# Moving the Wq and Wk loads to another queue, and four small reorderings ahead of them, in a kernel that sums a memory attention and an MLP

## The chip, the cores and the metric

The kernel runs on one core of one Trainium2 chip. The metric is the device time of one execution in microseconds (us). A core has TensorE (PE in the profile, with PEld for its weight loads), VectorE (DVE), ScalarE (ACT), GpSimd (POOL) and SyncE (SP). A DMA is started by an instruction in the queue of one of these engines, here SP or POOL, and every queue is worked off in order: an instruction that waits holds up all that stand behind it. The profile shows SP's own instructions as "SPq".

## The reference

Input x is 2048 rows of 1024 in bfloat16. Two branches work on its layer norm and are added to it.

```python
xn = _layernorm(x)
out = x + A(xn, mem0, Wq, Wk, Wv, Wo) + B(xn, w1, w2, w3, w4)

# A: 64 segments of 32 tokens, one after the other; 8 memory rows are carried along
for s in range(64):
    h = concat([mem, xn[32*s : 32*s+32]])             # 40 rows
    q, k, v = h @ Wq, h @ Wk, h @ Wv                  # 32 heads of 128
    p = softmax(where(mask, q @ k.T * 128**-0.5, -1e9))
    o = (p @ v) @ Wo
    mem, out_s = o[:8], o[8:]

# B
h  = gelu(layernorm(xn) @ w1)                         # 1024 -> 1024
hs = shift_tokens(h) @ w2                             # four column groups, shifted by +1, -1, +2, -2 rows
x1 = xn + hs
B  = x1 + gelu(layernorm(x1) @ w3) @ w4               # 1024 -> 3584 -> 1024
```

## The kernel before

The kernel doesn't carry the memory from segment to segment. It estimates the memory rows of all segments at once from sums over the segments, uses them for one parallel pass over all 2048 tokens, checks at the end that the rows which the pass gave agree with the estimate, and only if they don't runs a serial version (the branch behind line 868, not taken here). TensorE, SP and POOL work in the order in which the program is written; in the first two stages DVE and ACT do too.

1. **First MLP matmul (lines 222 to 363).** `load_x` (L233) and the quarters of w1 (L237) are queued on SP. For each of 16 tiles of 128 rows, `norm_stats` computes mean and variance on DVE (L256 for the left half, L259 for the right, L260, L261) and the inverse roots on POOL (L262). `norm2` makes the twice normed tile xn2 (L271 on DVE for tiles 0 to 7, L273 on ACT from tile 8). `transposes` turns tiles 0 to 7 on TensorE (L290) and copies them out (L294 on ACT, L292 on DVE for the second half of tile 0); later tiles are turned by a DMA (L274). `stage1` multiplies with w1 (L301), eight column blocks `co` of eight matmuls each, and runs gelu on ACT (L303). The dictionary `between` says after which `co` other work is put: `prep(n)` is norm2 of tile n, the statistics of n + 1 and the once normed tile n - 2 (L280, stored by L281). Tiles 0 to 3 go one at a time, then two at a time.
2. **Second MLP matmul (lines 365 to 391).** w2, layer norm of x1, transposed by DMA (L388).
3. **w3 and w4 (lines 393 to 556).** Four rounds `tb` over 512 rows each: 28 groups of eight matmuls with w3 (L522), then four row tiles of 56 matmuls with w4 (L545). At the start SP loads w4 in seven chunks (L418) between DMA transposes of xn (L409, `seg_sums`) whose sums over segments go into `xb` (L412). `mem_start` (L423 to L428) turns the 8 memory rows with eight small matmuls (L426), writes them into `MZ` (L427) and adds their sum to the first column of `xb` (L428). "Speculative" units (`spec_step`) are put between the big matmuls: `unit_vb` multiplies `xb` with Wv (L438) and is the first reader of `xb`. DVE adds each w4 product to `R1` (L546), which SP loads (L513) and POOL adds to x (L541).
4. **Values (lines 565 to 608).** All tokens times Wv (L577), written to memory (L584). At its end SP loads the weights of the first pass (L600) and Wq of the second (L603).
5. **Attention (lines 611 to 809).** Five blocks of 12 to 16 segments (4 tiles each, 5 in blocks 3 and 4), each with eight passes `hg` over four heads. A pass has eight projections, four with Wq and four with Wk (`proj`, L650, 64 matmuls together), and for every tile an "S" item and an "O" item. S (`scores`): four matmuls (L665), mask (L667), exp (L669), sums (L671), reciprocal (L673), product Pn (L677), and a DMA transpose PT<-Pn issued by SP (L680). O (`outputs`): four matmuls with the values V (L689), copied out by ACT (L690, L692). `tick` advances an estimated clock after each projection, starts S items when due and O items 10 us (`LAT`) after their S.
   The loads for a pass are made by `stage_loads` one pass ahead: two tiles `wt` from a pool of four (tag "w"), so that a load waits until TensorE has used the tile of two passes before; 512 KB halves (L737), then V (`load_values`, L635 to L643). They are put in a list `loads`, of which each `tick` issues one. After six of the eight projections of pass 1 of a block come the output projections of the block before (`Out.piece`, L708): for each of them POOL loads `Rt` (L706) and stores the result (L715), which waits for DVE (L714). At the start of pass 2, `block_setup` loads the next block's tokens `hTb` (L623) on POOL.

Of the kernel before, what the change touches and what calls it, by code (L numbers as in the profile page):

```python
# [77 lines left out]
def kernel(  # L78
# [16 lines left out]
    nc = tc.nc  # L95
# [6 lines left out]
    w1_v = B_w1.rearrange("(k p) n -> p k n", p=P)  # L102
# [90 lines left out]
    with tc.manual_schedule(engines={mybir.EngineType.PE, mybir.EngineType.SP, mybir.EngineType.Pool}), ExitStack() as actx:  # L193
# [6 lines left out]
        with ExitStack() as bctx:  # L200
# [13 lines left out]
            with ExitStack() as hctx:  # L214
# [7 lines left out]
                with ExitStack() as p0:  # L222
                    big = p0.enter_context(tc.tile_pool(name="p0big", bufs=1))
                    ring = p0.enter_context(tc.tile_pool(name="p0ring", bufs=3))
                    w1_sb = big.tile([P, KT, D], BF16)
# [4 lines left out]
                    def load_x(n):  # L230
                        if n < NT:
                            xts[n] = ring.tile([P, D], BF16, tag="xt", bufs=7, name=f"xt{n}")
                            nc.sync.dma_start(xts[n][:], x_v[:, n, :])  # L233

                    load_x(0)
                    for c0, c1 in ((0, 256), (256, 512), (512, 1024)):
                        nc.sync.dma_start(w1_sb[:, :, c0:c1], w1_v[:, :, c0:c1])  # L237
                        if c0 == 0:
                            load_x(1)
                    for n in range(2, 7):  # L240
                        load_x(n)
# [5 lines left out]
                    def norm_stats(n, part=None):  # L247

                        if n >= NT:
                            return  # L250
                        xt = xts[n]
                        if n not in stats:
                            stats[n] = [ring.tile(shape, F32, tag=tag, bufs=6, name=f"{tag}{n}") for tag, shape in (("st", [P, 2, 6]), ("mv", [P, 2]), ("ab", [P, 2]), ("rr", [P, 2]), ("nm2", [P, 1]))]
                        st, mv, ab, rr, nm2 = stats[n]
                        if part in (None, 0):
                            nc.vector.bn_stats(st[:, 0, :], xt[:, 0:512])  # L256
                        if part == 0:
                            return
                        nc.vector.bn_stats(st[:, 1, :], xt[:, 512:1024])  # L259
                        nc.vector.bn_aggr(mv[:], st[:])  # L260
                        nc.vector.scalar_tensor_tensor(ab[:], epsm[:], mv[:, 1:2], epsa[:], op0=ALU.mult, op1=ALU.add)  # L261
                        nc.gpsimd.tensor_tensor(rr[:], ab[:], neghalf[:], op=ALU.pow)  # L262
                        if n >= NPE:
                            nc.gpsimd.tensor_scalar(nm2[:], mv[:, 0:1], rr[:, 1:2], -1.0, op0=ALU.mult, op1=ALU.mult)
# [61 lines left out]
                    def tr(n, half, on_dve=False):  # L326
                        transposes(xn2s[n], tiles2[n - n % 2], n % 2, half, on_dve)
# [8 lines left out]
                    nc.gpsimd.memset(hTB[:, :, S + 2:S + 4], 0.0)  # L336
                    load_consts(4)
                    for n in range(1, NPE):
                        norm_stats(n + 1, 0)
                        norm2_of(n)  # L340
                        norm_stats(n + 1, 1)
                        if n > 1:
                            norm1(n - 2)
                        if n < 4:
                            stage1(n - 1, 1, tiles2[(n - 1) // 2 * 2], {5: [lambda n=n: tr(n, 0)], 6: [lambda n=n: tr(n, 1)]}, (n - 1) % 2)
                    stage1(3, 1, tiles2[2], {4: [lambda: tr(4, 0)], 5: [lambda: tr(4, 1)], 6: [lambda: tr(5, 0)], 7: [lambda: tr(5, 1)]}, 1)

                    def prep(n):
                        norm2_of(n)
                        norm_stats(n + 1)  # L350
                        norm1(n - 2)

                    for n0 in range(4, NT, 2):
                        between = {c: [] for c in range(KT)}
                        if n0 + 4 < NT:
                            between[2] += [lambda n0=n0: prep(n0 + 4)]
                            between[5] += [lambda n0=n0: prep(n0 + 5)]
                        if n0 == 4:
                            for c in range(4):
                                between[1 + 2 * c // 2 + (c > 1)] += [lambda c=c: tr(6 + c // 2, c % 2)]  # L360
                        stage1(n0, 2, tiles2[n0], between)
# [31 lines left out]
            with ExitStack() as p3:  # L393
# [29 lines left out]
                def mem_start():  # L423
                    ps9 = psum3.tile([P, KT, M + 1], F32, tag="vr")
                    for k in range(KT):
                        nc.tensor.matmul(ps9[:, k, :], m0[:, k * P:(k + 1) * P], eye9[:], start=True, stop=True)  # L426
                    nc.vector.tensor_copy(MZ[:, :, 0:M], ps9[:, :, 0:M])  # L427
                    nc.vector.tensor_tensor(xb[:, :, 0:1], ps9[:, :, M:M + 1], xb[:, :, 0:1], op=ALU.add)  # L428
# [59 lines left out]
                def spec_load(depth=1):  # L488
                    while units and len(pending) < depth:
                        u, i = units.pop(0)  # L490
                        pending.append(u(i))
                        if u is unit_g and i == 7:
                            pending.append(unit_thr)
# [23 lines left out]
                for tb in range(4):  # L517
                    depth = 1 if tb < 2 else 2
                    for f in range(FT):
                        ps = psum.tile([P, 512], F32, tag="mm", bufs=4)  # L520
                        for k in range(KT):
                            nc.tensor.matmul(ps[:].rearrange("p (n t) -> p n t", t=P), w3_sb[:, k, f * P:(f + 1) * P], xn3T[tb][:, :, k, :], start=(k == 0), stop=(k == KT - 1))  # L522
                        nc.scalar.activation(h3T[:, f, :], ps[:], ACTF.Gelu_apprx_tanh)  # L523
                        if tb > 0 and f % 7 == 6:
                            spec_step(depth)
                    if tb == 0:
                        spec_load()
                    if tb == 3:
                        w3ctx.close()
                        early = actx.enter_context(tc.tile_pool(name="aearly", bufs=2, side="right"))  # L530
                        vctx = ExitStack()
                        vph = vctx.enter_context(tc.tile_pool(name="vph", bufs=1, side="right"))
                        xT = vph.tile([P, NT, KT, P], BF16)
                    for j in range(4):
                        n = tb * 4 + j
                        R1, xt = r1s.pop(n)
                        load_r1(n + 1)
                        if tb == 3:
                            for m in range(4 * j, 4 * j + 4):
                                nc.sync.dma_start_transpose(xT[:, m], xn_v[:, m, :])  # L540
                        nc.gpsimd.tensor_tensor(R1[:], R1[:], xt[:], op=ALU.add)  # L541
                        for ch in range(2):
                            ps = psum.tile([P, 512], F32, tag="mm", bufs=4)
                            for f in range(FT):
                                nc.tensor.matmul(ps[:], h3T[:, f, j * P:(j + 1) * P], w4_sb[:, f, ch * 512:(ch + 1) * 512], start=(f == 0), stop=(f == FT - 1))  # L545
                            nc.vector.tensor_tensor(R1[:, ch * 512:(ch + 1) * 512], ps[:], R1[:, ch * 512:(ch + 1) * 512], op=ALU.add)  # L546
                        if n == NT - 1:
                            while pending or units:
                                spec_step(depth)
                        elif n > 0:  # L550
                            spec_step(depth)
                        else:
                            mem_start()
                        if n == NT - 2:
                            load_wv()
                        nc.gpsimd.dma_start(R_v[:, n, :], R1[:])
# [8 lines left out]
            for hg in range(8):  # L565
                cs_ = slice(hg * 512, (hg + 1) * 512)
# [155 lines left out]
        loads = []  # L722
# [5 lines left out]
        def stage_loads(Bs, hg, ready=()):  # L728

            cs_ = slice(hg * 512, (hg + 1) * 512)  # L730
            ws = [(w, None) for w in ready]
            ws += [(wtile(), src) for src in (Wq_v, Wk_v)[len(ready):]]
            (wq, _), (wk, _) = ws
            Vs = [qkv.tile([P, len(B["tiles"]), 512], BF16, tag="V", bufs=3, name=f"V{B['b']}") for B in Bs]
            for w, src in ws[len(ready):]:
                for k0 in (0, 4):
                    loads.append(lambda w=w, src=src, k0=k0: nc.sync.dma_start(w[:, k0:k0 + 4, :], src[:, k0:k0 + 4, cs_]))  # L737
            for B, V in zip(Bs, Vs):
                loads.append(lambda B=B, V=V: load_values(B, V, hg))
            return wq, wk, Vs  # L740
# [21 lines left out]
        for gi_, group in enumerate(groups):  # L762
# [3 lines left out]
            for hg in range(8):  # L766
                cs_ = slice(hg * 512, (hg + 1) * 512)
# [100 lines left out]
    with tc.If(cond > 0):  # L868
        with ExitStack() as fctx:
# [18 lines left out]
            with tc.For_i(0, NSEG, 1) as i:  # L888
# [6 lines left out]
                for hg in range(8):  # L895
                    cs_ = slice(hg * 512, (hg + 1) * 512)
# [100 lines left out]
```

## Time and profile before

| | |
|---|---|
| median of 7 runs | 1527.56 us (1526.19 to 1532.76) |
| the profiled execution's own time | 1526.44 us |
| its span, first to last instruction | 1524.5 us |
| TensorE busy | 1513.4 us of the span; granted clock 0.999 |
| DVE, ACT, POOL busy | 545.9, 506.3, 178.9 us |
| matmuls of the attention: L650, L708 | 509.5, 225.2 us busy |
| matmuls of the values: L577 | 221.2 us busy |
| matmuls of the MLP: L522, L545 | 195.5, 196.0 us busy |
| DMA | 274.20 MB, mean 180 GB/s |

The span is what the trace covers; 1.9 us of the profiled execution's time lie outside it. Times inside the trace are counted from the start of the span. "Idle before" an instruction is the time for which its engine had nothing in work, and the name behind the arrow is what ended it. A matmul's end is modelled and about 0.17 us later than the point at which the next matmul can start, so that the time lost in a gap of TensorE is better taken from start to start, less the regular step between two matmuls of the same shape (0.216 us for 512 columns, by the 1024 of L577 in 221.2 us, and about 0.055 us for 128 columns).

### The profile page before, as it was taken

Reading aid. Unit: us, or ns where it says so; the run is one execution under the profiler, and the core shown is the slowest. Engines: PE = TensorE matmul, PEld = TensorE weight load, DVE = VectorE, ACT = ScalarE, POOL = GpSimd, SP = SyncE. Lnnn points to the kernel's source line nnn. Section 1 sums busy time; section 2 is a strip of 40 time slices with the busy share of each in tenths; the row PEclk is TensorE's granted clock in tenths of the full one; section 3 lists DMA queues with packets and bytes.
Section 4 is the critical chain, followed back from the end, with each engine's and each line's share of the span. In section 5 each row is a group of like instructions: output and inputs, shape, how many; then the busy total and the mean of one; then the engine's idle time right before and its main releaser. Section 6 shows DMA issues by size and latency. Waiting matters only on the chain.

```text
span 1524.5 us, 24352 instructions
## 1 busy us (share of the span) xinstructions
PE 1513.4 (99%) x9853; PEld 809.0 (53%) x9853; DVE 545.9 (36%) x1137; ACT 506.3 (33%) x1147; POOL 178.9 (12%) x248
## 2 busy tenths in 40 slices
PE   9999999999999999999999999999999999999998
PEld 7844444444444444444465645664665555445555
DVE  7383320000200122211145624650664266416542
ACT  5533203103012011111256614650663266326630
POOL 5232030221211231100000010001000100010001
PEclk9999999999999999999999999999999999999999
DMA  8799963452452977532499956992997389828611
GB/s 267 172 251 298 246 213 118 146 187 83 145 156 75 235 259 256 204 123 79 131 245 236 242 129 177 241 236 78 242 234 196 110 223 215 193 72 212 174 44 55
DMA packets 305435, 274.20 MB, mean 180 GB/s; under 512 B 153787, under 2 KB 273104, under 8 KB 305064
## 3 DMA queue, kind: packets, MB, share of 16 engines
q1 hardware_dynamic: 283144, 189.92, 49.8%
q0 software_dynamic: 22032, 82.63, 15.5%
q8 instruction: 79, 1.29, 0.4%
q14 instruction: 36, 0.29, 0.1%
q10 hardware_dynamic: 144, 0.07, 0.0%
HBM read 190.98 MB, written 46.19 MB: 156 GB/s over the span
## 4 chain that ended last, share of the span: by engine, by line
PE 93%; SPq 3%; DMA 3%; DVE 0%; ACT 0%; issue 0%; POOL 0%; POOLq 0%; DVEq 0%
PE ps L650 30%; PE pso L708 15%; PE ps L577 14%; PE ps L545 11%; PE ps L522 10%; PE ps L375 4%; PE ps L301 3%; SPq L409 2%; PE psS L665 2%; PE psO L689 2%; DMA PT<-Pn 1%; DMA xp<-xn_scratch 1%; PE ps L837 1%; PE ps L473 1%; DMA xt<-in_A_x_dram 1%; PE ps L438 1%
## 5 line engine op out<-in xcount | busy, mean ns | idle before, releaser
L650 PE MATMUL ps<-hTb,wt 128*128 128x396 bf16 (+3 forms) x2560 | 509.5, 343 | 0.0
L650 PEld LDWEIGHTS <-wt 128*128 128x128 bf16 x2560 | 234.1, 97 | 166.1
L708 PE MATMUL pso<-wo_sb,oX 128*128 128x512 bf16 (+1 forms) x1056 | 225.2, 373 | 0.0
L577 PE MATMUL ps<-wt,xT 128*128 128x512 bf16 x1024 | 221.2, 379 | 0.0
L545 PE MATMUL ps<-w_sb,h3T 128*128 128x512 bf16 x896 | 196.0, 379 | 0.4 <-DMA w_sb<-in_B_w_dram 0.4
L522 PE MATMUL ps<-xn3T,w_sb 128*128 128x512 bf16 x896 | 195.5, 379 | 0.0
L577 PEld LDWEIGHTS <-xT 128*128 128x128 bf16 x1024 | 100.2, 98 | 120.8
L523 ACT ACTIVATE h3T<-ps 128x512 bf16<-128x512 f32 x112 | 66.8, 597 | 291.8 <-PE ps L522 290.9
L708 PEld LDWEIGHTS <-oX 128*128 128x128 bf16 x1056 | 102.0, 98 | 112.4
L656 ACT CAST KT<-ps 128x396 bf16<-128x396 f32 (+3 forms) x160 | 82.1, 513 | 224.3 <-PE ps L650 222.5
L522 PEld LDWEIGHTS <-w_sb 128*128 128x128 bf16 x896 | 86.9, 98 | 102.9
L545 PEld LDWEIGHTS <-h3T 128*128 128x128 bf16 x896 | 86.7, 98 | 103.1 <-issue 0.6
L671 DVE TENSOR_REDUCE sums<-sm 99x4 f32<-99x396 f32 (+2 forms) x176 | 97.6, 555 | 113.2 <-ACT sm L669 113.2
L667 DVE TENSOR_TENSOR sm<-psS,c_mask_reg_sb 99x396 f32<-99x396 f32 x160 | 91.3, 570 | 92.2 <-PE psS L665 91.7
L669 ACT ACTIVATE sm<-sm 99x396 f32<-99x396 f32 (+2 forms) x176 | 92.8, 527 | 71.4 <-DVE sm L667 70.8
L579 ACT CAST Vs<-ps 128x512 bf16<-128x512 f32 x64 | 37.4, 585 | 233.2 <-PE ps L577 233.2
L658 ACT ACTIVATE QT<-ps 128x396 bf16<-128x396 f32 (+3 forms) x160 | 84.1, 526 | 74.1 <-PE ps L650 55.0
L583 DVE CAST Vs<-ps 128x512 bf16<-128x512 f32 x64 | 44.3, 692 | 170.0 <-PE ps L577 166.4
L677 DVE TENSOR_TENSOR Pn<-sm,rs 99x396 bf16<-99x396 f32 (+2 forms) x176 | 98.9, 562 | 6.9 <-DMA PT<-Pn 0.9
L546 DVE TENSOR_TENSOR R<-ps,R 128x512 f32<-128x512 f32 x32 | 21.8, 690 | 200.3 <-PE ps L545 169.2
L690 ACT CAST oX<-psO 128x384 bf16<-128x384 f32 (+1 forms) x176 | 82.5, 469 | 10.3 <-PE psO L689 9.8
L715 POOL DMA_DIRECT2D out_dram<-ot x30 | 16.3, 544 | 585.7 <-DVE ot L714 579.9
(115 smaller groups left out, 981.5 us busy)
## 6 DMA issues: line engine op xcount, KB each, us to landing
wt<-in_A_Wk_dram SPq DMA_DIRECT2D x78, 512.0 KB
wt<-in_A_Wq_dram SPq DMA_DIRECT2D x76, 512.0 KB
wt<-in_A_Wv_dram POOLq DMA_DIRECT2D x24, 1024.0 KB, 6.7
V_scratch<-Vs SPq DMA_DIRECT2D x32, 512.0 KB
V<-V_scratch SPq DMA_DIRECT2D x32, 384.0 KB
w_sb<-in_B_w_dram SPq DMA_DIRECT2D x8, 1024.0 KB
R_scratch<-x POOLq DMA_DIRECT2D x16, 512.0 KB, 4.2
R<-R_scratch SPq DMA_DIRECT2D x16, 512.0 KB
```

What stands on the lines that cost most here:

```text
L522: nc.tensor.matmul(ps[:].rearrange("p (n t) -> p n t", t=P), w3_sb[:, k, f * P:(f + 1) * P], xn3T[tb][:, :, k, :], start=(k == 0), stop=(k ...
L545: nc.tensor.matmul(ps[:], h3T[:, f, j * P:(j + 1) * P], w4_sb[:, f, ch * 512:(ch + 1) * 512], start=(f == 0), stop=(f == FT - 1))
L577: nc.tensor.matmul(ps[:], xT[:, m4 * 4 + j, k, :], wv[:, k, :], start=(k == 0), stop=(k == KT - 1))
L650: nc.tensor.matmul(ps[:, :nb] if flat else ps[:, :nb].rearrange("p (t c) -> p t c", t=nt), w[:, k, hh * P:(hh + 1) * P], B["rhs"](k), star ...
L656: nc.scalar.copy(o, i)
L658: nc.scalar.mul(o, i, scale)
L667: nc.vector.tensor_tensor(sm[:T, :, :T], S3, t["mask"][:].unsqueeze(1).to_broadcast((T, 4, T)), op=ALU.add)
L669: nc.scalar.activation(e[:T, :, :T], sm[:T, :, :T], ACTF.Exp, scale=LN2)
L671: nc.vector.tensor_reduce(ss, e[:T, :, :T], axis=AX.X, op=ALU.add)
L677: nc.vector.tensor_tensor(Pn[:T, :, :T], e[:T, :, :T], rs[:T, :].unsqueeze(2).to_broadcast((T, 4, T)), op=ALU.mult)
L690: nc.scalar.copy(oX[:, hs_, at:at + nt], O3[:, :, 0:nt])
L708: nc.tensor.matmul(self.ps[:, :self.w], self.oX[:, h, self.gl * P:(self.gl + 1) * P], wo_sb[:, h, self.cc], start=(h == 0), stop=(h == H - 1))
```

## The change

There are five edits. The first four are in the MLP, the last in the attention.

- w1 is loaded in four quarters of 256 columns; before, it was two quarters and a half. The second tile of x is queued after the second quarter, before after the first.
- For tile 1, the statistics of tile 2 (both halves) come after norm2 of tile 1. Before, those of the left half of tile 2 came ahead of it.
- From the second pair of tiles on (`n0` from 6), `prep` is put one `co` earlier (after 1 and 4, before after 2 and 5).
- `mem_start` comes after the last w3 group of the first round, before it came after the first w4 tile.
- The loads of Wq and Wk at L737 are issued by POOL, before by SP. Those at L600 and L603 stay on SP.

```diff
                     load_x(0)
-                    for c0, c1 in ((0, 256), (256, 512), (512, 1024)):
-                        nc.sync.dma_start(w1_sb[:, :, c0:c1], w1_v[:, :, c0:c1])
-                        if c0 == 0:
+                    for c in range(4):
+                        nc.sync.dma_start(w1_sb[:, :, c * 256:(c + 1) * 256], w1_v[:, :, c * 256:(c + 1) * 256])
+                        if c == 1:
                             load_x(1)
...
                     for n in range(1, NPE):
-                        norm_stats(n + 1, 0)
+                        if n > 1:
+                            norm_stats(n + 1, 0)
                         norm2_of(n)
-                        norm_stats(n + 1, 1)
+                        norm_stats(n + 1, 1 if n > 1 else None)
...
                         if n0 + 4 < NT:
-                            between[2] += [lambda n0=n0: prep(n0 + 4)]
-                            between[5] += [lambda n0=n0: prep(n0 + 5)]
+                            between[1 + (n0 == 4)] += [lambda n0=n0: prep(n0 + 4)]
+                            between[4 + (n0 == 4)] += [lambda n0=n0: prep(n0 + 5)]
...
                     if tb == 0:
+                        mem_start()
                         spec_load()
...
                         elif n > 0:
                             spec_step(depth)
-                        else:
-                            mem_start()
...
             for w, src in ws[len(ready):]:
                 for k0 in (0, 4):
-                    loads.append(lambda w=w, src=src, k0=k0: nc.sync.dma_start(w[:, k0:k0 + 4, :], src[:, k0:k0 + 4, cs_]))
+                    loads.append(lambda w=w, src=src, k0=k0: nc.gpsimd.dma_start(w[:, k0:k0 + 4, :], src[:, k0:k0 + 4, cs_]))
```

In the changed program's order of instructions, TensorE has the same matmuls in the same order but for the eight of L426; DVE differs in the place of one L256 and of L427 and L428 (now ahead of the last two L412); ACT in the places of L273; SP has 154 weight loads of the attention fewer, which POOL has instead, and one load of w1 more. On POOL, the weight loads of a pass stand one behind the other with nothing between them but `hTb` at pass 2, and those of pass 3 of blocks 1 to 4 stand behind the six pairs of `Rt` load and result store of that block.

## The prediction

> **What bounds the kernel now.** I read the page first, then what TensorE waited for, then its timeline at each such place with those of DVE and SP beside it.
>
> ```profile
> span 1524.5 us, 24352 instructions
> PE 1513.4 (99%) x9853; PEld 809.0 (53%) x9853; DVE 545.9 (36%) x1137; ACT 506.3 (33%) x1147; POOL 178.9 (12%) x248
> q1 hardware_dynamic: 283144, 189.92, 49.8%
> q0 software_dynamic: 22032, 82.63, 15.5%
> ```
>
> TensorE is busy for 99% of the span and its matmuls stay the same, so the change can only win gaps. The two queue lines matter later: SP's queue q1 moves 671 bytes a packet (189.92 MB by 283144), POOL's q0 3750. All that TensorE waits for:
>
> ```profile
> PE psO L689 <- DMA PT<-Pn: 2.4, 2, 1.2
> PE warm L318 <- DVE wz L312: 1.4, 1, 1.4
> PE ps L301 <- DMA w_sb<-in_B_w_dram: 1.1, 1, 1.1
> PE ps L290 <- DVE xn L271: 0.8, 1, 0.8
> PE ps L438 <- DVE xb L428: 0.7, 1, 0.7
> PE ps L301 <- ACT xn2T L294: 0.5, 1, 0.5
> PE ps L545 <- DMA w_sb<-in_B_w_dram: 0.4, 1, 0.4
> ```
>
> That is 7.3 us; 5.4 of them stand where the five edits act (not L312, not L294). Counted from start to start, less the regular step, the six gaps there cost 1.23, 0.94, 0.52, 0.91, 1.39 and 1.30, together 6.3 us: the ceiling of any gain. In order of time, from the timelines of TensorE and DVE:
>
> ```profile
> 11.71 1.07 PE L301 MATMUL ps<-xn2T,w_sb 128*128 128x128 bf16 x16 [1.06 <-DMA w_sb<-in_B_w_dram]
> 12.35 0.69 DVE L256 BATCH_NORM_STATS2 st<-xt 128x6 f32<-128x512 bf16 x1 [2.38 <-DMA xt<-in_A_x_dram]
> 12.96 0.53 DVE L271 TENSOR_SCALAR xn<-xt,mv,rr 128x1024 bf16<-128x1024 bf16 x1
> 13.55 0.40 PE L290 MATMUL ps<-c_ident_sb,xn 128*128 128x128 bf16 x4 [0.77 <-DVE xn L271]
> ...
> 180.53 7.07 PE L545 MATMUL ps<-w_sb,h3T 128*128 128x512 bf16 x32 [0.35 <-DMA w_sb<-in_B_w_dram]
> 187.53 0.35 PE L426 MATMUL ps<-c_eye_sb,m 8*128 8x9 bf16 x8
> 200.58 0.18 DVE L428 TENSOR_TENSOR xb<-ps,xb 128x8 bf16<-128x8 f32 x1
> 200.82 1.09 PE L438 MATMUL ps<-xb,wt 128*128 128x64 bf16 x32 [0.74 <-DVE xb L428]
> ```
>
> At 11.7 TensorE waits for the half of w1; DVE holds tile 1's norm (L271) back behind tile 2's statistics, whose x has not come. At 180 the last chunk of w4 is late; at 200 L428 stands on DVE behind two L546 that waited for R1. The third place is in passes 2 and 3 of block 0 (802.30 and 816.02 on TensorE), where SP's timeline reads:
>
> ```profile
> 790.06 1.25 SPq L680 DMA_TRANSPOSE PT<-Pn  x1
> 791.37 1.66 SPq L737 DMA_DIRECT2D wt<-in_A_Wk_dram  x1
> 793.34 0.63 SPq L635 DMA_DIRECT2D V<-V_scratch  x1
> 794.02 0.41 SPq L637 DMA_DIRECT2D V<-Vmem_scratch  x1
> 794.48 0.25 SPq L638 DMA_DIRECT2D V<-Vmem_scratch  x1
> 794.83 4.75 SPq L680 DMA_TRANSPOSE PT<-Pn  x2
> ```
>
> The transpose is ready when Pn is (793.05) but goes at 794.83, behind half a Wk and a V in SP's queue and then behind their bytes.
>
> **What the Trainium skill says.** "DMA: Bandwidth & Descriptors", section "Issuing engines are not separate DMA queues": all queues run on the same 16 engines, and another issuer saves only issue time. Section "Queues, rings and completion order": an engine takes the queues in turn, a packet each. Section "SWDGE vs HWDGE vs iDMA": POOL's packets are made up to 4096 bytes. The trace agrees with the last (3750 on average, and most q0 records are of 4096), so that in a contest POOL's weights get 4096 bytes for each 256 of a transpose. "SBUF — State Buffer", section "SBUF: two separate sides": POOL can't write descriptors while DVE runs certain SBUF-to-SBUF operations. The trace shows no such delay in the attention, where POOL's issues take 0.54 us (L715).
>
> **The change part by part.**
>
> *w1 and tile 2's statistics.* The third quarter of w1 now has 2.1 MB ahead of its end (two of x, three quarters) and not 2.6 as the half had. At the 290 to 350 GB/s that the DMA shows from 2 to 10 us, it comes 1.5 to 1.8 us sooner, so the 1.06 goes. What is late next is x tile 1, now behind one quarter more: 0.52 MB, 1.5 to 1.8 us. Before, L256 took it at 6.93 without waiting; in the packet records its last packet ends between 6.5 and 7.0. I take 8.5. On DVE the copy L292 of tile 0 is queued behind that L256; it ended at 8.87 and will at about 9.85, and TensorE's fifth matmul needs it. So L301 stands for 1.0 us after four matmuls, then runs 44 more at 0.055 and is at tile 1's L290 at 12.3. DVE and POOL beside it: L259 at 9.8, roots done 1.96 later (8.79 to 10.75 before), L271 at 11.8 with no tile 2 ahead, L290 0.59 later at 12.4. It was 13.55: **1.15 gained**. Bounds: x tile 1 with no delay lets TensorE arrive at 11.3 (2.2 gained, all there is); a quarter taking 2.5 us gives 13.3 (0.25). Tile 2's norm is then at about 15.2 (15.43 before), needed at 12.4 + 4.2 = 16.6: covered. A loss here would need x tile 1 after 9.6; excluded by the rates.
>
> *prep one co earlier.* In order ACT's L273 could block gelu, but each waits for roots made 4 to 6 us earlier (tile 10: ready 38.5 by POOL's L264, used at 39.41, now 38.5; later ones over 3 us). TensorE runs 336 matmuls there without a gap: 0, hidden by that. If tile 10's were late, PSUM's four buffers cover 2.6 us.
>
> *mem_start.* Its eight matmuls move from 187.5 to before the first L545; the 0.35 us stay. They now fill part of the wait for w4, whose time SP's queue sets: about 0.4 of 0.52 gained. On DVE, L427 and L428 stand before the last pair of L412, ready at 190, and xb is complete at 194.84 with the last L412, 5 us ahead of L438. Its 0.91 goes, but for 0.1 that any switch to small matmuls shows. L545's PSUM buffer is freed at 199.94, before L438 ends. **1.2 gained**; bounds 0.8 and 1.4.
>
> *Wq and Wk on POOL.* SP loses four issues of 0.4 to 0.6 us in each 12.3 us pass, and their bytes no longer stand ahead of the transposes in q1. POOL has time for 154 at about 0.6, 92 us. There each load waits only for its tile, so it starts when TensorE is through with the tile of two passes before, half a pass or more sooner; SP paced it. Both late transposes become early: **2.7 gained**. Upper bound, nothing else waits for PT. For the lower bound: an O item starts 7.75 us after Pn in the even passes, and 1.15 of that go between last packet and matmul (least seen), so a transpose may take 6.6. Alone it takes 1.8. Beside a POOL load of 1 MB, the nearest row is L477 at 449.52, 462.65 and 475.78: the last packet is 5.7 to 5.8 us after issue, with 512 packets to PT's 448, so about 5.4. That is below 6.6; nothing new waits. Some passes could: lower bound in the second rival. Next, pass 3's weights after each output stage. POOL is held in L715 until 923.5, then hTb (852 KB), then Wq (1.05 MB). hTb took 6.6 us to land, Wq adds 3.9 at the 269 GB/s of a pass: 934, needed 938.0. No stall, 4 us spare; four times.
>
> *Sum.* 1.15 + 1.2 + 2.7 = 5.05. The profiled execution took 1526.44 (span 1524.5 and 1.9 outside), so 1521.4; the median is 1.12 higher, so **1522.5**.
>
> **The rivals.** (a) *The transposes were late for lack of bandwidth, not for their place in the queue.* For it: DMA is busy 85 to 115% in the passes; the skill says that another issuer adds nothing. Against: only 197 to 275 GB/s move there, and 350 to 389 at the start. The 2.7 stay: 1527.56 - 2.35 = 1525.2. (b) *POOL's packets crowd out SP's.* Place: the transpose behind V in a pass. V is 24 packets of 1 KB on each engine; with one of 4096 bytes (0.159 us in the records) after each it takes 24 x 0.205 = 4.9 us, the transpose 3.3 more, with 1.2 of issue 9.4 after Pn where 6.6 is allowed: 2.8 of stall. Against it: a load alone lasts about 3 us of each 6 and seldom covers both. It decides from two such passes on; at 5 of the 39 passes, 14 us: 1527.56 - 2.35 + 14 = 1539.2, slower. (c) *Pass 3's weights come late* because POOL sits in L715: 2 us at the three outputs with an hTb behind: 1522.5 + 6 = 1528.5.
>
> **How the numbers follow.** Forecast 66%, (a) 18%, (b) 11%, (c) 5%. About 0.2%, 3.05 us, is what a measurement of this kernel can tell. The forecast's own range is 1521.3 (6.3 gained) to 1525.0 (0.25 + 0.8 + 1.5), by the bounds of the first two terms and 1.5 to 2.7 for the third; 64 of its 66% are faster by over 3.05. Then 64% faster, 25% within (2 + 18 + 5), 11% slower. The range, 1520.2 to 1526.5, takes in the forecast and (a) with a microsecond for the scatter of medians; (b), (c) stay out.
>
> **What would show it.** Right: L290 of tile 1 near 12.4 with a new wait of about 1 us near 8.8; no wait of L438 on L428; no wait of L689 on PT; SP free of L737. Wrong: waits of L689 on PT anywhere in the passes (b), of L650 on wt after an output stage (c), or the two in block 0 unchanged (a).

## The result, and the profile after

The changed kernel takes 1541.75 us (median of 25 runs, 1536.36 to 1550.09), the kernel before 1527.9 beside it: a ratio of 1.0079, 95% interval 1.0065 to 1.0093. By the medians it is slower by 13.9 us, by the ratio by 12.1; 5 us less than before had been predicted. The profiled execution took 1544.8, 3 us more than the median. The page after, lines that answer to those of before:

```profile
span 1542.9 us, 24380 instructions
...
PE 1518.5 (98%) x9853; PEld 810.5 (53%) x9853; DVE 546.0 (35%) x1137; ACT 506.9 (33%) x1147; POOL 293.7 (19%) x402
...
q0 software_dynamic: 44208, 163.38, 34.0%
q1 hardware_dynamic: 202872, 109.17, 31.9%
```

81 MB went from q1 to q0, as meant. TensorE has the same 9853 matmuls but is busy for 5.1 us more: some ran slower. What it waited for:

```profile
PE psO L689 <- DMA PT<-Pn: 14.8, 7, 6.9
...
PE ps L301 <- DVE xn2T L292: 1.2, 1, 1.2
PE ps L547 <- DVE R L548: 1.1, 1, 1.1
```

Two waits for PT with 2.4 us have become seven with 14.8. By stage, from the first matmul of the attention (L650): it begins at 759.7 before and 759.9 after, so in these two profiles the MLP edits brought nothing up to there; the attention lasts 764.8 before and 782.9 after. Of these 18.1 us, waits for PT make 13.3 (16.0 less the 2.7 of before, start to start) and slower matmuls about 4.5. Passes 1, 2 and 3 of block 0 took 19.1, 15.4 and 18.7 us, before 11.9, 12.4 and 13.8; nearly all others are unchanged. (Passes are counted from 0, each from its first L650 to that of the next; counted so, the two waits of before lie in passes 3 and 4, where the prediction says 2 and 3.) In the same 12 us (PE, PEld, DVE, ACT and POOL busy with counts, granted clock of TensorE, DMA share, GB/s), before and then after:

```profile
783.00:795.00 12.00, 12.00 (x95) 7.61 (x94) 7.72 (x18) 7.80 (x21) 0.00 (x0) 1.00 1.04 234
```

```profile
783.00:795.00 12.00, 5.36 (x22) 2.85 (x23) 2.64 (x6) 2.15 (x6) 1.33 (x2) 0.59 1.05 199
```

The DMA is as busy as before and moves less. TensorE stands for 6.9 us, and its clock is 0.5 from 785.17 to 795.41, which makes the mean of 0.59 in this stretch. On TensorE, on POOL and on SP at that place, after:

```profile
789.64 0.51 PE L689 MATMUL psO<-PT,V 106*128 106x106 bf16 x4 [6.91 <-DMA PT<-Pn]
789.95 2.90 PE L650 MATMUL ps<-hTb,wt 128*128 128x403 bf16 x8
```

```profile
771.34 1.49 POOL L737 DMA_DIRECT2D wt<-in_A_Wk_dram  x2 [3.96 <-PE ps L650]
772.82 0.55 POOL L623 DMA_DIRECT2D hTb<-hT_scratch  x1
777.19 1.49 POOL L737 DMA_DIRECT2D wt<-in_A_Wq_dram  x2 [3.82 <-PE ps L650]
782.85 1.49 POOL L737 DMA_DIRECT2D wt<-in_A_Wk_dram  x2 [4.17 <-PE psS L665]
```

```profile
775.38 4.01 SPq L680 DMA_TRANSPOSE PT<-Pn  x2
```

SP issues the first two transposes of the block at once (775.38 and 778.19, 0.07 us after their Pn), with no weights ahead: that part of the edit works. But POOL issues 4.0 MB between 771 and 785, of which up to 2.95 MB are under way at once (issued and not yet landed), and the first three PT land 10.6, 10.7 and 14.7 us after their Pn (last packet, from the trace's packet records). Eight matmuls of L650 take 2.90 us where they take 1.53 at full clock. The second POOL line is also new: before, `hTb` of block 1 ran here:

```profile
650.50 0.56 POOL L623 DMA_DIRECT2D hTb<-hT_scratch  x1
```

In POOL's order it now stands behind the weights of pass 2, and its 0.85 MB moved by 122 us, in among the first transposes.

### The profile page after: what moved, and what is told of

Its sections match the earlier page's. It is cut to its first block, busy times and chain, and to the rows that moved or that the text cites. A ratio compares the mean times of both kernels' runs of the same rounds, so it can differ in the third digit from the quotient of the medians.

```text
span 1542.9 us, 24380 instructions
## 1 busy us (share of the span) xinstructions
PE 1518.5 (98%) x9853; PEld 810.5 (53%) x9853; DVE 546.0 (35%) x1137; ACT 506.9 (33%) x1147; POOL 293.7 (19%) x402
## 4 chain that ended last, share of the span: by engine, by line
PE 88%; DMA 6%; SPq 3%; DVE 2%; ACT 1%; issue 0%; POOL 0%; POOLq 0%; DVEq 0%; ACTq 0%
PE ps L650 27%; PE pso L708 14%; PE ps L577 14%; PE ps L547 11%; PE ps L523 9%; DMA PT<-Pn 4%; PE ps L376 4%; SPq L410 2%; PE ps L301 2%; PE psO L689 2%; PE psS L665 2%; DMA xp<-xn_scratch 1%; PE ps L837 1%; PE ps L474 1%; PE gps L453 0%; PE ps L439 0%
## 5 line engine op out<-in xcount | busy, mean ns | idle before, releaser
L650 PE MATMUL ps<-hTb,wt 128*128 128x396 bf16 (+3 forms) x2560 | 513.4, 345 | 0.0
L650 PEld LDWEIGHTS <-wt 128*128 128x128 bf16 x2560 | 235.4, 98 | 168.1 <-issue 3.4
L737 POOL DMA_DIRECT2D wt<-in_A_Wk_dram x78 | 58.1, 749 | 292.2 <-PE psO L689 120.4
L548 DVE TENSOR_TENSOR R<-ps,R 128x512 f32<-128x512 f32 x32 | 21.8, 690 | 199.3 <-PE ps L547 168.3
L737 POOL DMA_DIRECT2D wt<-in_A_Wq_dram x76 | 56.6, 750 | 179.4 <-PE psO L689 105.2
```

The source lines that it names most:

```text
L650: nc.tensor.matmul(ps[:, :nb] if flat else ps[:, :nb].rearrange("p (t c) -> p t c", t=nt), w[:, k, hh * P:(hh + 1) * P], B["rhs"](k), star ...
L737: loads.append(lambda w=w, src=src, k0=k0: nc.gpsimd.dma_start(w[:, k0:k0 + 4, :], src[:, k0:k0 + 4, cs_]))
```

## The experiments

Each time is a median, with the ratio to the kernel before on the same chip and its 95% interval; "over before" is the difference of the two medians, and need not agree with the ratio to the last microsecond. "Landing" is the time from Pn to the last packet of its PT, over the 168 full transposes: 3.34 us in the median before (4 over 6.6, the allowance of the prediction), 4.61 after (15 over 6.6). Landings and waits are those of each run's one profiled execution. Diffs are against the kernel after unless said, and shortened ("...").

### Which edit

**The weight loads alone** (kernel before with the one edit):

```diff
-loads.append(lambda ...: nc.sync.dma_start(w[:, k0:k0 + 4, :], src[:, k0:k0 + 4, cs_]))
+loads.append(lambda ...: nc.gpsimd.dma_start(w[:, k0:k0 + 4, :], src[:, k0:k0 + 4, cs_]))
```

> Only the queue of the Wq and Wk loads is changed, the MLP is that of before. The theory: the whole loss comes from this edit; TensorE waits for late transposes (L689 on PT) at the start of block 0 for some 11 us, a few shorter ones later, and the clock is halved for a while after the first long wait. Expected 1540 to 1546 us. If the MLP edits took part in the loss, this run stays below 1536.

1541.31 us, 1.009 (1.0056 to 1.0124), 13.5 over before. Landing 4.73, 13 over 6.6. The whole loss is this edit's.

**The four MLP edits alone** (L737 back on SP):

> Only the four MLP edits; Wq and Wk stay on SP. Theory: they win their gaps and give the time back at the next limit (ACT's wait for POOL at tile 8, the addition of R1 in the first w4 tiles), as L577 starts at nearly the same time in both traces; the two waits of block 0 stay. Expected 1526.5 to 1528.5, no measurable change. The prediction's sum for these edits was a gain of 2.35, so 1525.3.

1526.32 us, 0.9992 (0.9979 to 1.0006): no change that the runs can tell, though the predicted gain of 2.35 us (0.9985) lies inside the interval too. Its waits:

```profile
PE psO L689 <- DMA PT<-Pn: 1.2, 1, 1.2
PE ps L301 <- DVE xn2T L292: 0.9, 1, 0.9
PE ps L301 <- ACT xn2T L294: 0.8, 2, 0.5
```

The first MLP matmul has the new waits of the kernel after; the wait at the R tile isn't there in this profile.

### Queue, packets, early start

**ACT's queue** (kernel before, with `nc.scalar.dma_start` at L737). It takes the weights off SP as POOL does, with packets of 1 KB:

> MLP of before, loads on ScalarE's queue, the third way to take them out of SP's: paced by ScalarE's own order, and with packets of 1 KB as on SP. If place in SP's queue was the cause of the two waits of block 0, they go and the time is 1524 to 1526 us; if bandwidth was, they stay and it is 1527 to 1529. ScalarE has 0.5 us of issue four times a pass of 12.3 us, of which it is busy 8: if that delays the copies out, TensorE waits for PSUM or for exp and the time is above 1530.

1529.6 us, 0.9988 (0.9964 to 1.0012): by the medians 1.8 us more, by the ratio 1.8 less, so neither loss nor gain. Its weight queue on the page, and its waits for PT (the first is listed under "issue"):

```profile
q10 hardware_dynamic: 81456, 80.82, 21.7%
```

```profile
PE psO L689 <- issue: 1.5, 1, 1.5
...
PE psO L689 <- DMA PT<-Pn: 1.0, 2, 0.8
```

992 bytes a packet (80.82 MB by 81456), landing 3.91, 2 over 6.6. About as much waiting is left as before. Of the two old waits one is left with 0.8 us and the other is gone; the one of 1.5 is new, in pass 1. No weights stand ahead of the transposes in SP's queue now, but V still does: the transpose of the wait that is left went 1.48 us after its Pn, behind V (before 1.78, behind half a Wk and V), while that of the new wait went at once (0.06). So the place behind the weights was not what made them late, or not alone. Nor does an early start alone cost time: ACT's loads too begin up to 10 us sooner than SP's did. How much a transpose suffers from packets beside it, from the packet records of all full transposes (packets of the weight queue that end between its first and its last packet):

```
packets beside a PT      0 to 19        20 to 149       150 and more
POOL, 4096 bytes      0.74 us (99)    2.12 us (66)    5.29 us (3)
ACT, 1 KB             0.52 us (80)    1.39 us (52)    1.98 us (36)
```

(median time from the first to the last packet of a PT, number of PT in brackets; a PT is 448 packets of 256 bytes.) The POOL row is the kernel after, the ACT row this run. More than 150 packets of 1 KB cost less than 20 to 149 of 4096. But the count depends on the time, as a longer transpose sees more packets; and in bytes the second POOL group (median 96 packets) had 0.39 MB beside it, the third ACT group (median 224) only 0.23. So the table fits queues that take turns by packets, but doesn't prove it. Such turns stand in the Trainium skill, "DMA: Bandwidth & Descriptors", section "Queues, rings and completion order". Queue and packet size changed together here; there is no run of POOL with packets of 1 KB, so the two are not told apart.

**POOL held back** (kernel before, weights on POOL, each load behind a POOL copy from the last projection's output, so that it goes about when SP's did or later: at the start of the attention at most 2.2 us sooner, where the kernel after was up to 11 us sooner):

```diff
+def paced(w, src, k0, cs_):
+    nc.gpsimd.tensor_copy(pace[:], last[0])
+    nc.gpsimd.dma_start(w[:, k0:k0 + 4, :], src[:, k0:k0 + 4, cs_])
...
+            last[0] = dst[:, hh, 0:1]
...
-                    loads.append(lambda ...: nc.sync.dma_start(w[:, k0:k0 + 4, :], src[:, k0:k0 + 4, cs_]))
+                    loads.append(lambda ...: paced(w, src, k0, cs_))
```

> MLP of before, loads on POOL, but each load is held until the projection after which it stands is copied out (POOL copies one column of that copy first), so that POOL can't run a pass ahead. Two theories of the late transposes. Piling up: POOL runs ahead, so that in passes 1 to 3 of block 0 several loads and hTb stand back to back in its queue and starve the transposes; then pacing brings nearly all of it back, 1526 to 1531 us, and L689 waits under 3 us. Share: any POOL load beside a transpose makes it late because of the packet sizes; then pacing changes little, 1538 us or more, with waits spread over all blocks.

1552.49 us, 1.0159 (1.012 to 1.0197), 24.7 over before; landing 5.17, 26 over 6.6, in a profile that is the quickest of its four runs (1542.54). The loss doesn't need the early start; held to about the old times, POOL hurts more. Block 1's `hTb` is displaced here too, to 778.64.

**Block 0's weights on SP**, the others on POOL:

```diff
-loads.append(lambda ...: nc.gpsimd.dma_start(w[:, k0:k0 + 4, :], src[:, k0:k0 + 4, cs_]))
+loads.append(lambda ...: (nc.sync if Bs[0]["b"] == 0 else nc.gpsimd).dma_start(w[:, k0:k0 + 4, :], src[:, k0:k0 + 4, cs_]))
```

> The changed kernel, with Wq and Wk of block 0 issued by SP as before and those of blocks 1 to 4 by POOL. Theory: nearly all of the loss stands in passes 1 to 3 of block 0, 12.3 us of PT waits and about 4.5 us of matmuls at half clock after them; without them the 4 us of later waits stay and the time is 1527 to 1530. Rival: the first block to get its weights from POOL shows it, whichever it is; then passes 1 to 3 of block 1 take 4 us or more longer than before and the time is 1535 or more.

1541.36 us, 1.0092 (1.0059 to 1.0125): the rival's number, not the theory's, though not at the rival's place, which was passes 1 to 3 of block 1. Passes 1 to 3 of block 0 are as before (11.9, 12.4, 14.0 us), and pass 7, in which POOL's first loads meet SP's last, takes 24.3 (before 12.4). On POOL and TensorE there, its first load and the longer of two waits:

```profile
840.05 1.49 POOL L737 DMA_DIRECT2D wt<-in_A_Wq_dram  x2 [190.65 <-DMA PT<-Pn]
861.78 0.49 PE L689 MATMUL psO<-PT,V 99*128 99x99 bf16 x4 [5.89 <-DMA PT<-Pn]
```

Block 0 is nothing special: it pays where POOL's loads begin. Four transposes land there 8.7 to 14.3 us after their Pn, with at most 2.1 MB of POOL's under way, but SP's last four halves and POOL's first four, 4.2 MB together, are issued within 12 us. No `hTb` is near (block 1's ran at 648.84), so that one alone doesn't explain the loss either.

### The displaced hTb and the backlog

**hTb of block 1 set up at pass 0**, so that POOL loads it ahead of all weights:

```diff
-if hg == 2 and gi_ + 1 < len(groups):
+if hg == (2 if gi_ else 0) and gi_ + 1 < len(groups):
```

> The changed kernel, with the tokens of block 1 (hTb) set up at pass 0 of block 0 instead of pass 2, so that their load stands ahead of all weight loads in POOL's order. In the kernel before it ran at 650 us, in the values stage, because nothing stood ahead of it; in the changed kernel it stands behind the weights of pass 2 and ran at 773 us, among the transposes of block 0. If that displaced 0.85 MB is what makes passes 1 to 3 of block 0 late, the long waits there go and the time is 1529 to 1532. If weights in large packets and POOL's running ahead are enough, 2 to 4 us of the 18 go and the time is 1537 to 1540.

1536.15 us, 1.0055 (1.0023 to 1.0087), 8.7 over before. Passes 1 to 3 of block 0 are 12.1, 12.4 and 15.3 us, but waits of 0.2 to 3.1 us stand all over the attention. About 5 of the 13.9 us are hTb's; a little better than the second expectation.

**The same, held back** (the paced kernel with hTb early):

> The kernel before, with the weight loads on POOL, each held until the last projection has been copied out (paced), and hTb of block 1 ahead of them all. Together with the changed kernel, the paced one and the one with hTb early it makes a table of two by two. If POOL's early start and hTb only hurt together, this one has no wait over 3 us in block 0 and takes 1530 to 1533; if the share of the large packets is enough by itself, PT waits of 6 us and more stay in block 0 and the time is 1540 or more.

1547.13 us, 1.0144 (1.0109 to 1.018), but its four runs go from 1533.77 to 1553.32 and the profiled one is the quickest, with no long wait in block 0 and one of 4.3 in block 2. The profile doesn't show the median's loss; only that holding back doesn't help, as above. Over before it is 19.7 us, 5.1 less than the paced kernel with hTb late: the early hTb takes off about 5 us here as it does without holding back.

**Loads of 128 KB**, one tick each, so that V comes later in a pass:

```diff
-for k0 in (0, 4):
-    loads.append(lambda ...: nc.gpsimd.dma_start(w[:, k0:k0 + 4, :], src[:, k0:k0 + 4, cs_]))
+for k0 in range(8):
+    loads.append(lambda ...: nc.gpsimd.dma_start(w[:, k0:k0 + 1, :], src[:, k0:k0 + 1, cs_]))
```

> The changed kernel, with each half of Wq or Wk loaded by POOL as four DMAs of 128 KB with one row of 1 KB for each partition, where it was one of 512 KB with four rows. If packets of POOL come out at 1 KB so, the packet theory wants the share of a load to fall fourfold: no wait over 3 us, PT waits of 2 to 4 us together, 1527 to 1531, as with ACT's queue. If POOL itself is the cause (its queue, its way of making descriptors), the time stays at 1540 or more with packets of 1 KB. If the packets stay near 4096 bytes, the run tells nothing between the two, and the time should stay at 1540.

1531.98 us, 1.0034 (1.0013 to 1.0055), 5.1 over before. The packets stayed at 4096 bytes (38080 of them, as after), yet 9 of the 13.9 us are gone: the third expectation missed. Since V had moved too, **128 KB with V in its place**:

```diff
-loads.append(lambda ...: nc.gpsimd.dma_start(w[:, k0:k0 + 4, :], src[:, k0:k0 + 4, cs_]))
+loads.append(lambda ...: [nc.gpsimd.dma_start(w[:, k:k + 1, :], src[:, k:k + 1, cs_]) for k in range(k0, k0 + 4)])
```

> The changed kernel, with each 512 KB half issued as four DMAs of 128 KB in the same tick, so that V keeps its place in SP's order. POOL can then issue no more than 128 KB in each 0.54 us or more and keeps fewer bytes ready. If the backlog in POOL's queue is what the transposes stand beside, the time is near that of the run with V moved as well, 1530 to 1535. If V's place behind two more transposes made that gain, the time stays at 1539 to 1543.

1535.59 us, 1.0053 (1.0034 to 1.0073), 8.0 over before. POOL's timeline shows a likely reason why small loads are milder:

```profile
771.12 1.60 POOL L737 DMA_DIRECT2D wt<-in_A_Wq_dram  x3 [3.08 <-DMA wt<-in_A_Wk_dram]
...
778.35 3.18 POOL L737 DMA_DIRECT2D wt<-in_A_Wk_dram  x6 [1.54 <-DMA wt<-in_A_Wq_dram]
```

In this program POOL's DMAs report their landing on eight semaphores in turn, so each waits until the eighth before it has landed: eight loads of 128 KB are 1 MB. And a load of 128 KB takes 0.54 us to issue where 512 KB take 0.75. So less is under way: in the first passes at most 1.77 MB with hTb, where it was 2.95. Landing is 3.76, but a PT wait of 5.0 us stays. So splitting the loads takes off some 6 us, and the smaller backlog (what is under way at once) is the likely reason; V's place may be 2.9 more, but the two intervals overlap.

**Both, 128 KB loads and hTb early**:

> The changed kernel with 128 KB loads, V in its place, and hTb of block 1 ahead of all weights. If backlog and the displaced hTb add up (hTb early alone took 5.6 us off), 1526 to 1530. If they are the same microseconds, no better than the better of the two alone: 1531 to 1536.

1532.24 us, 1.0024 (1.0004 to 1.0044), 4.6 over before: the loss is down to a third. Single savings of 5 and 6 make 9 together. PT waits of 7.8 us, the longest of 2.3, stay in the profile, which is 5 us slower than the median.

### The plan of the O items

**MLP edits, loads on SP, `LAT = 12.0`**:

```diff
-        LAT = 10.0
+        LAT = 12.0
```

> The four edits of the MLP, the weight loads on SP as in the kernel before, and the O items planned 12 us after their S item, where it was 10. If the two late transposes of the kernel before lack only 1.2 to 1.4 us, their waits (2.7 us, or 1.4 in the kernel with the MLP edits alone) go at no cost: 1524 to 1525, a ratio of 0.997 to 0.998. Rival: planning O items later moves waits to the ends of the blocks, where items pile up behind the last projections, or to the S items; then 1527 to 1530.

1523.49 us (23 runs), 0.9978 (0.9967 to 0.999): 3.4 us quicker than the kernel before and the best of all. How much of it is the plan's isn't told, as this interval overlaps that of the MLP edits alone. Its profiled execution is its slowest (1541.29, with one 13.4 us wait for w4) and is read only for this: one wait for PT, 0.4 us. **The same with 13**:

> The four edits of the MLP, the weight loads on SP, and the O items planned 13 us after their S item. It tells whether the 1593 us of the changed kernel with 13 us come from the plan or from the plan with POOL's loads. If the plan alone is at fault (O items then end after the V load of two passes later is issued, which waits for them in SP's queue, ahead of the transposes), this one too is slower than 1540, with waits of SP at L635. If it takes POOL's loads as well, it stays at 1524 to 1530.

1527.23 us, 1.0004 (0.9987 to 1.0021). No wait for PT, but 2.2 us for Wq, and landing is later (4.47, 35 over 6.6). The plan alone costs nothing.

**The kernel after with 13 and with 12**:

> The changed kernel with the O items planned 13 us after their S item, where it was 10. Theory (POOL's 4096-byte packets take turns with the 256-byte packets of the transposes, so PT lands 4.6 us after Pn in the median and up to 14.7 in block 0): three more microseconds cover all but the landings over about 9.6 us, so of the 16.3 us of waits 5 to 8 stay and the time is near 1532. The landings themselves stay as late. Rival (the loss is not lateness of PT but what POOL's traffic does elsewhere, or a shift of the order of items): the time stays at 1540 or more. A second rival: five PT buffers are too few for 13 us, the S items are held up and the gain is lost again, with waits on other operands than PT.

> The changed kernel with the O items planned 12 us after their S item, 2 us more than in it and 1 less than in the one that took 1593 us. With the loads on SP 12 us took 1523.5. If lateness of PT against its O item is what costs, and 12 us is still short of the trouble that 13 us made, a third to a half of the PT waits goes: 1532 to 1537. If a later O item makes the transposes later still beside POOL's loads, as the 70 landings over 6.6 us with 13 us suggest, it is slower than the changed kernel: over 1545.

1593.36 us, 1.042 (1.0387 to 1.0452), and 1581.92 us, 1.0263 (1.0203 to 1.0323; the four runs with 12 go from 1560.37 to 1592.57, and the ratio takes the two quickest). More slack made it far worse: with 13 the expectation was missed by 60 us, with 12 the second one held. The profile with 13:

```profile
PE psO L689 <- DMA PT<-Pn: 53.9, 22, 7.0
```

Its two worst passes, of 21.8 and 26.2 us, come shortly after output stages, where POOL has been held at L715 and then lets go of everything:

```profile
937.73 0.53 POOL L623 DMA_DIRECT2D hTb<-hT_scratch  x1
938.25 1.50 POOL L737 DMA_DIRECT2D wt<-in_A_Wq_dram  x2
939.74 1.49 POOL L737 DMA_DIRECT2D wt<-in_A_Wk_dram  x2
```

The same burst stands in the kernel after at 939.04 to 942.55. There Pn of that pass came 5.8 us behind the hTb issue (944.87) and its first five PT landed in 4.0 to 6.6 us; with 13 it came 2.8 us behind (940.48), in the middle of the burst, and they took 9.5 to 13.2. At this place the plan shifted the transposes onto the burst. **128 KB loads, hTb early and 12**:

> As e14_128k_htb, with the O items planned 12 us after their S item. With 512 KB loads this plan took 1582, with loads on SP 1523.5. If the long waits need a backlog of POOL's packets, 1523 to 1532. If any POOL load does it, 1550 or more.

1537.19 us, 1.007 (1.0049 to 1.0092): between the two expectations, 45 us better than with 512 KB loads and hTb late, yet 5 us worse than the same kernel with 10. The longest wait for PT in its profile (1529.02, the quickest of five) is 1.7 us. So most of what the later plan costs goes with the 512 KB loads or the late hTb; which of the two isn't told.

## Why the prediction was wrong

- **Wq and Wk (2.7 gained): failed.** The step is "Beside a POOL load of 1 MB, the nearest row is L477 ... so about 5.4. That is below 6.6; nothing new waits". It priced one transpose beside one load. At the start of block 0 three transposes, one behind the other and V between, stood beside 4.0 MB that POOL issued within 14 us: they took 10.6, 10.7 and 14.7. Over the whole attention 4.61 is the median and inside the 5.4; it is the few late ones that stall TensorE.
- **The lateness of before, "behind half a Wk and a V in SP's queue": at most half right.** With ACT's queue there were no weights in SP's, and about as much waiting was left, as rival (a) would have it; but V was still in SP's queue, ahead of the one transpose whose old wait was left, so how much the place does isn't settled. In the profile with two more microseconds in the plan one wait of 0.4 us is left.
- **hTb** was priced only behind L715. That the same load of block 1 ran at 650.50 and would fall behind L737 was in POOL's timeline and order, and was overlooked: about 5 us. The edit moved nothing of this load, but put new ones ahead of it. Its packets in q0 are of 6656 bytes, more than the "up to 4096" of the working.
- **Rival (b), 11%**: transposes late beside POOL's loads came as it said, and its 1539.2 was only 2.6 us short, which is luck in part: whether the packets do it isn't shown, and place and price were not as told: not 5 of 39 passes with 2.8 us each but mainly waits of 7.1 and 4.7 us at the start of block 0, and a term it lacked, matmuls at half clock (about 4.5 us). Its "against" ("a load alone lasts about 3 us of each 6") fails when loads follow one another, and its 3.3 us for the transpose is too little by its own rule: 28 packets an engine with one of 0.159 us after each are over 4.4.
- **Rival (c)**: no wait of L650 for wt after an output stage. The burst there did no harm in this kernel; with a later plan it did the most.
- **w1 and tile 2's statistics (1.15 gained): right at its place, then given back.** L290 of tile 1 came at 12.46 (12.4 predicted, 13.55 before), the new wait was 1.20 (1.0). But at tile 8 TensorE met ACT. On TensorE, and on ACT before and after:

```profile
9.99 2.62 PE L301 MATMUL ps<-xn2T,w_sb 128*128 128x128 bf16 x44 [1.20 <-DVE xn2T L292]
12.46 0.40 PE L290 MATMUL ps<-c_ident_sb,xn 128*128 128x128 bf16 x4
...
33.89 0.38 PE L290 MATMUL ps<-c_ident_sb,xn 128*128 128x128 bf16 x4 [0.62 <-ACT xn2T L294]
...
36.81 1.36 PE L301 MATMUL ps<-xn2T,w_sb 128*128 128x256 bf16 x11 [0.35 <-ACT xn2T L294]
```

```profile
32.06 1.24 ACT L273 ACTIVATE xn<-xt,nm,rr 128x1024 bf16<-128x1024 bf16 x1 [0.34 <-POOL nm L264]
```

```profile
32.13 1.24 ACT L273 ACTIVATE xn<-xt,nm,rr 128x1024 bf16<-128x1024 bf16 x1 [1.50 <-POOL nm L264]
```

  The last two waits cost 0.78 and 0.52, start to start. ACT had waited for roots (L273 behind L264) for 0.34 and now waits 1.50: the roots are no earlier than before. The other profiles say the same: over the five with the old MLP and the twelve with the new, L290 of tile 1 starts at 13.33 and 12.19 in the median, the second MLP matmul at 71.24 and 71.15. The failed words are "each waits for roots made 4 to 6 us earlier"; tile 8 was not looked at.
- **mem_start (1.2 gained): mostly not.** L438's wait on L428 is gone as said; w4 gained 0.16, not 0.4. But the product after it waits for R1: "L545's PSUM buffer is freed at 199.94" held for the kernel before; in this profile SP came to R1 1.55 us later (193.18, before 191.63):

```profile
202.04 2.32 PE L547 MATMUL ps<-w_sb,h3T 128*128 128x512 bf16 x10 [1.13 <-DVE R L548]
```

  This place scatters: six of the twelve profiles with the new MLP have the wait for R1 (0.6 to 1.9 us), the one with the MLP edits alone has not; of the five with the old MLP two have no wait of L438, and with the weights on ACT it stood for 3.1. The attention begins at 758.0 to 762.3 with the old MLP and, but for one profile with a wait of 13.4 us for w4, at 758.0 to 760.8 with the new. Why SP was later is open.

What stays open: whether POOL's packets of 4096 bytes or POOL's queue as such does it; how much V in SP's queue adds; the last 4.6 us with small loads and hTb early; and why holding POOL back costs 11 us more.

## What to carry to other kernels

A load is not only issued elsewhere when its queue changes: its packets and its backlog can change too. Before moving prefetches beside small latency-bound transfers, look at bytes per packet of both queues, at how much the new queue can have outstanding at once, and at which loads of its own fall behind the newcomers. Here late small transfers were cheaper to cover in the plan of the consumer (two microseconds later, 3.4 us gained together with the MLP edits) than by rearranging queues, and only as long as no burst of loads stood where the plan moves them.

## What the runs showed of the hardware

- A stall of TensorE can halve its clock, from within the stall on and for a while after it: the trace grants 0.5 from 785.17 to 795.41, around the wait that ended at 789.64, and from 815.89 to 819.30, around the one that ended at 816.06. The Trainium skill, "TensorE: Matmul & The Clock Gate", section "What's actually happening", has the two states and a free-running window of about 3.4 us, with which the traces agree: these stretches are three windows and one of 3.41, and all four changes lie on one grid of that step. The page asks for a whole idle window; here less was enough. In the 17 profiles, from 8.5 us on and up to the last 3 us, all 31 falls of the clock stand at the end of such a window in which TensorE had stood for 2.1 us or more (2.13 to 3.41), and the 87 windows in which it stood for 1.0 to 2.15 us kept the full clock (idle time counted from start to start, less the regular step). So the length of a wait alone doesn't decide: a wait of 2.4 us with block 0's weights on SP halved the clock, one of 3.1 us with the weights on ACT fell across two windows and didn't.
- Single packets stand for over 1 us, often many at the same moment: in the attention up to 2.7 us in the kernel before, 4.2 in the kernel after, 5.6 at most in all runs. In the kernel before, eight packets of 1 KB of q1 that began at 794.2 to 794.4 took 2.2 to 2.4 us, some time ahead of the wait for PT that ended at 802.30. In the attention some 380 packets took over 1 us before, 509 after, some 880 with `LAT` 13 beside POOL's loads. In that last run, with POOL's burst and transposes both queued, the core moved only 79 and 48 GB/s in the two stretches of 2 us from 960 on. What holds the packets isn't shown.
- A POOL load of 512 KB took 0.75 us of POOL to issue, one of 128 KB 0.54: the 462 further DMAs of the 128 KB loads raised POOL's busy time from 294 to 506 us, beside other work.
